# Six more attention heads with scores split in two terms, and the weights' low parts moved from GpSimd to VectorE

## The chip, the cores and the metric

The kernel runs on one core of a Trainium2 chip. Its engines are TensorE (PE in the profile, with PEld for its weight loads), VectorE (DVE), ScalarE (ACT), GpSimd (POOL) and SyncE (SP, which issues most DMAs here). Each engine has its own queue of instructions, and the engines wait for one another through semaphores. The metric is the device time of one execution in microseconds; lower is better.

## The reference

Eight batches of eight heads of causal attention with a decay, over 576 positions with 64 elements a head, then one two-layer network over all 4608 rows. All of it is in float32.

```python
scores = scale * np.matmul(q, k.transpose(0, 1, 3, 2))
cum = np.cumsum(np.log(np.clip(f, 0.0001, 1.0)), axis=-1)
scores = np.where(causal, -1e9, scores + cum[..., :, None] - cum[..., None, :])
attn = exp(scores - max(scores)) / (sum + 1e-09)
x = matmul(attn, v)                      # 64 heads of 576 x 64, heads side by side: 4608 x 512
h = np.maximum(x @ w_in, 0.0)            # w_in 512 x 2048, given as float64
out = h * h @ w_out                      # w_out 2048 x 512, given as float64
```

The kernel receives the two weight matrices as float64 words and turns them into float32 itself.

## The kernel before

**Attention.** A head is worked in six *units* (score tiles: keys in tiles of 128 on the partitions, queries along the free axis, in the shapes 128x320, 128x320, 128x192, 66x64, 128x448 and 128x256). The program runs over *slots*, one unit of one head each: 64 heads x 6 units, with some slots ahead of the first head. In a slot stand, in this order: the unit's `score` matmuls with the exponential on ScalarE (`p`), the product of `p` with `v` for the unit of two slots before (`av_part`), the steps of the division (`finish`), and then twice (half 0 and half 1 of the slot): events with due times, a stretch of weight conversion (`cv`), and as many halves of a network step as `fill` says are due. The events of half 0 stand ahead of the first stretch and those of half 1 ahead of the second.

**Maxima.** A softmax needs each query's maximum ahead of its scores. `max_units(h)` computes rough scores one head ahead, in six pieces: one matmul of the rounded q (`r2`, the stationary operand) and rounded k (`kl0`), and one reduction on VectorE that writes the negative maximum per query. The table `MAXIMA` holds their slots, for whole and for split heads.

**Whole and split heads.** `NWHOLE` says which heads are *whole*: for these, q and k are loaded twice by DMA (rounded on the way into `rk` by `load_rounded`, and as they are into `rl` by `load_whole`), a unit's scores are one float32 matmul pair (two records in the profile), the mask is added by a small bf16 matmul, `p` and `v` are used as float32, and the six maxima are gathered in a column tile, turned into a row by five small matmuls and copied by ScalarE (`turn_maxima`). For the *split* heads, q and k come once as `qkraw`; `prep` makes rounded high parts and low parts (the remainder, another subtraction), a unit's scores are two single-pass matmuls in fp32r (high by high with the decay and maximum rows, and a second one over 128 rows that holds both cross terms), the maxima go to their row by small DMAs, and `p` and `v` are split too, with three matmuls each. Before the change, heads 0 to 15 are whole and heads 16 to 63 are split.

**Weights.** `weight_ops` converts 32 tiles of 128x512 weights in four yields each: VectorE clips and shifts the exponent and joins the words (lines 228, 233, 236 and 240), ScalarE makes the magnitude (line 205) and the rounded high part (line 210), and GpSimd subtracts it for the low part (line 216, one yield ahead of line 240 of the following tile). `RATES` gives yields per slot.

**Network.** A step of it has two halves. `mlp1` multiplies a chunk of 256 rows by one tile of `w_in` (12 matmuls, line 555), then ScalarE makes relu and square (`r`, `gh`) and VectorE the exact square and its low part (`g`, `gl`). `mlp2` multiplies by a tile of `w_out` (6 matmuls, line 578), one step behind. The network of a batch of heads runs in between the attention of the next batch, so that of batch 0 runs beside heads 8 to 15; after the last head only network is left. When the second chunk of rows begins, scores and maxima share two PSUM banks; before that they have four.

**Order.** `in_order` ties PE, ACT, DVE and POOL to the order in which the program was traced; SP's DMAs are placed by the scheduler. So on these four an instruction that waits holds up all that stands behind it.

## Time and profile before

| | us |
|---|---|
| time, median of 3 runs | 1220.62 (1219.54 to 1220.74) |
| profiled execution, its own time | 1217.56 |
| its span, first to last instruction | 1215.8 |
| mean granted TensorE clock | 0.994 of full speed |
| busy: PE, DVE, ACT, POOL | 1189.4, 769.5, 706.2, 361.8 |

By place of the span: up to about 95 us only attention and weight conversion run (heads 0 to 8); from there to about 230 us heads 9 to 15 with the network of batch 0 and the rest of the conversion; then heads 16 to 63 with the network of the batch before; from about 1057 us only network. In rows of instructions, the first number is the start in us from the span's beginning, the second how long the record lasts; successive records of one engine overlap, so that the cost of one is read from its start to the start of the next. "x2" joins two records. A bracket at a row's end gives how long the engine sat idle ahead of it, and what ended that.

### The profile page before, as it was taken

Reading aid. Unit: us, or ns where it says so; the run is one execution under the profiler, and the core shown is the slowest. Engines: PE = TensorE matmul, PEld = TensorE weight load, DVE = VectorE, ACT = ScalarE, POOL = GpSimd, SP = SyncE. Lnnn points to the kernel's source line nnn. Section 1 sums busy time; section 2 is a strip of 40 time slices with the busy share of each in tenths; the row PEclk is TensorE's granted clock in tenths of the full one; section 3 lists DMA queues with packets and bytes.
Section 4 is the critical chain, followed back from the end, with each engine's and each line's share of the span. In section 5 each row is a group of like instructions: output and inputs, shape, how many; then the busy total and the mean of one; then the engine's idle time right before and its main releaser. Section 6 shows DMA issues by size and latency. Waiting matters only on the chain.

```text
span 1215.8 us, 23255 instructions
## 1 busy us (share of the span) xinstructions
PE 1189.4 (98%) x7816; PEld 1047.3 (86%) x7816; DVE 769.5 (63%) x2031; ACT 706.2 (58%) x1736; POOL 361.8 (30%) x551
## 2 busy tenths in 40 slices
PE   6999999899999999999999999999999999999998
PEld 3668787779999898999999989988999899999997
DVE  5767776766767667665655766667676767533332
ACT  3875556566666666655556566666666666533232
POOL 3332322333334333322322333333333333200000
PEclk8999999999999999999999999999999999999999
DMA  7889310111211112111121212212121212000000
GB/s 217 206 198 272 90 42 26 47 46 42 59 42 53 38 47 50 41 49 27 43 55 21 53 32 44 57 42 58 37 50 33 58 43 58 12 28 11 9 18 18
DMA packets 104767, 72.16 MB, mean 59 GB/s; under 512 B 86573, under 2 KB 86573, under 8 KB 104649
## 3 DMA queue, kind: packets, MB, share of 16 engines
q1 hardware_dynamic: 103368, 65.96, 21.2%
q0 software_dynamic: 1280, 4.72, 1.6%
q8 instruction: 62, 1.02, 0.4%
q14 instruction: 57, 0.46, 0.1%
HBM read 60.51 MB, written 9.87 MB: 58 GB/s over the span
## 4 chain that ended last, share of the span: by engine, by line
PE 90%; ACT 4%; DVE 2%; issue 2%; DMA 1%; POOL 0%; SPq 0%; DVEq 0%; POOLq 0%; ACTq 0%
PE bank L555 33%; PE bank L578 31%; PE bank L346 4%; PE bank L392 3%; PE bank L435 3%; PE bank L456 3%; PE bank L402 3%; PE bank L437 3%; PE bank L436 3%; PE bank L399 3%; ACT r L563 1%; DVE bank L354 1%; ACT gh L565 0%; ACT den L471 0%; ACT p L409 0%
## 5 line engine op out<-in xcount | busy, mean ns | idle before, releaser
L578 PE MATMUL bank<-w,gh 128*128 128x512 f32 x1152 | 414.1, 400 | 0.0
L555 PE MATMUL bank<-xh,w 128*128 128x256 f32 x2304 | 329.0, 285 | 1.9 <-POOL w L216 1.9
L555 PEld LDWEIGHTS bank<-xh,w 128*128 128x128 f32 x2304 | 300.3, 189 | 10.3 <-POOL w L216 2.4
L425 DVE TENSOR_TENSOR pl<-p,ph 128x320 fp32r<-128x320 f32 (+4 forms) x288 | 177.4, 616 | 192.8 <-ACT ph L424 188.3
L578 PEld LDWEIGHTS bank<-w,gh 128*128 128x128 f32 x1152 | 217.5, 189 | 38.4
L563 ACT ACTIVATE r<-bank 128x256 f32<-128x256 f32 x288 | 110.6, 384 | 218.4 <-PE bank L555 172.3
L578 PE MATMUL bank<-w,gl 128*128 128x512 f32 x576 | 226.9, 394 | 0.2 <-DVE gl L566 0.2
L564 DVE TENSOR_TENSOR g<-r 128x256 f32<-128x256 f32 x288 | 125.7, 437 | 146.6 <-ACT r L563 146.0
L424 ACT CAST ph<-p 128x320 fp32r<-128x320 f32 (+4 forms) x288 | 119.4, 415 | 145.6 <-POOL p L411 103.0
L411 POOL TENSOR_SCALAR_AFFINE_SELECT p<-p 128x128 f32<-128x128 f32 (+1 forms) x240 | 77.1, 321 | 412.0 <-ACT p L409 317.6
L555 PE MATMUL bank<-xl,w 128*128 128x256 f32 x1152 | 184.5, 282 | 0.0
L555 PEld LDWEIGHTS bank<-xl,w 128*128 128x128 f32 x1152 | 158.2, 191 | 0.2 <-DVE xl L543 0.2
L566 DVE TENSOR_TENSOR gl<-g,gh 128x256 fp32r<-128x256 f32 x288 | 130.3, 452 | 36.2 <-ACT p L409 2.0
L354 DVE CUSTOM_DVE_ANT_0 bank<-bank,mz 128x256 f32<-128x256 f32 (+4 forms) x320 | 133.4, 433 | 22.6 <-PE bank L346 20.5
L409 ACT ACTIVATE p<-bank 128x320 f32<-128x320 f32 (+4 forms) x288 | 111.6, 388 | 60.1 <-PE bank L402 48.9
L565 ACT ACTIVATE gh<-r 128x256 fp32r<-128x256 f32 x288 | 120.6, 419 | 9.4
L346 PE MATMUL bank<-rk 66*128 66x320 f32 (+4 forms) x384 | 110.6, 317 | 13.9 <-DVE tcol L354 11.0
L578 PEld LDWEIGHTS bank<-w,gl 128*128 128x128 f32 x576 | 109.3, 190 | 14.4 <-DVE gl L566 0.9
L435 PE MATMUL bank<-pl,vh 128*65 128x320 f32 (+4 forms) x336 | 93.3, 278 | 2.6 <-ACT den L471 2.6
L346 PEld LDWEIGHTS bank<-rk 66*128 66x128 f32 (+1 forms) x384 | 67.2, 181 | 29.3 <-DVE tcol L354 13.0
L436 PE MATMUL bank<-ph,v 128*64 128x320 f32 (+4 forms) x336 | 91.2, 271 | 0.0
L437 PE MATMUL bank<-ph,vh 128*65 128x320 f32 (+4 forms) x336 | 89.3, 272 | 0.0
(92 smaller groups left out, 1539.0 us busy)
## 6 DMA issues: line engine op xcount, KB each, us to landing
qkraw<-in_qk SPq DMA_DIRECT2D x48, 288.0 KB
v<-in_v SPq DMA_DIRECT2D x64, 160.0 KB
out<-osb SPq DMA_DIRECT2D x36, 256.0 KB
den<-rdr SPq DMA_DIRECT2D x62, 144.0 KB
w<-in_w_in SPq DMA_DIRECT2D x16, 512.0 KB
w<-in_w_out SPq DMA_DIRECT2D x16, 512.0 KB
rl<-in_qk SPq DMA_DIRECT2D x16, 288.0 KB
rk<-in_qk POOLq DMA_DIRECT2D x16, 288.0 KB, 4.4
```

What stands on the lines that cost most here:

```text
L346: nc.tensor.matmul(ps[:m, :n], st["r2"][:D + 2, q0:q0 + m], st["kl0"][:D + 2, k0:k0 + n], start=True, stop=True,)
L354: nc.vector.tensor_tensor_reduce(out=ps[:m, :n], in0=ps[:m, :n], in1=mz[:m, mo:mo + n], op0=ALU.add, op1=ALU.min, scale=-1.0, scalar=init, ...
L425: nc.vector.tensor_tensor(out=pl[:kn, :n], in0=p[:kn, :n], in1=ph[:kn, :n].bitcast(F32), op=ALU.subtract,)
L435: nc.tensor.matmul(acc[:D + 1, o], vh, pl[:kn, i], start=first, stop=False)
L436: nc.tensor.matmul(acc[:D, o], vl, ph[:kn, i], start=False, stop=False)
L437: nc.tensor.matmul(acc[:D + 1, o], vh, ph[:kn, i], start=False, stop=last)
L555: nc.tensor.matmul(ph[:, :T], w[:, s, cc], x[:, cc, :], start=(cc == 0 and k == 0), stop=(cc == NCC - 1 and k == 2),)
L563: nc.scalar.activation(out=r, in_=ph[:, :T], func=AF.Relu)
L564: nc.vector.tensor_tensor(out=g, in0=r, in1=r, op=ALU.mult)
L565: nc.scalar.activation(out=gh, in_=r, func=AF.Square)
L566: nc.vector.tensor_tensor(out=gl, in0=g, in1=gh.bitcast(F32), op=ALU.subtract)
L578: nc.tensor.matmul(po, g[:, ts], w[:, s], start=(fc == 0 and k == 0), stop=(fc == NF - 1 and k == 2),)
```

## The change

Heads 10 to 15 become a third kind. They have split scores like the later heads (`prep`, two matmuls a unit, maxima by small DMAs, and the later due times of `MAXIMA`: from slot 1.5 to slot 4 of the head before, where whole heads have slot 0 to slot 2.5), but `p` and `v` stay whole and the mask is added by a matmul, as in whole heads. Their `prep` differs from that of the later heads: the rounded k (part 0, slot 0.5) and the rounded q (part 1, slot 1.5) are cast by ScalarE straight into `rk`, copied from there into `rl` by a DMA from SBUF to SBUF, and both low parts are subtracted on VectorE (parts 2 and 3, slots 1.5 and 3.5). The old `prep`, with the casts for `rk` on VectorE at slot 0.5 and the low parts on GpSimd, is now `prep_split` and serves heads 16 to 63. In the weight conversion, the low part moves from GpSimd to VectorE and one yield later, behind line 240.

```diff
-    NWHOLE = 16
+    NWHOLE = 10
+    NPLAIN = 16
...
         def low_part(i):
...
-                nc.gpsimd.tensor_tensor(out=hl[:, 1], in0=w, in1=hl[:, 0].bitcast(F32), op=ALU.subtract)
+                nc.vector.tensor_tensor(out=hl[:, 1], in0=w, in1=hl[:, 0].bitcast(F32), op=ALU.subtract)
...
             nc.vector.scalar_tensor_tensor(wi, high, -0x40000000, wi, ALU.bitwise_and, ALU.bitwise_or)
-            low_part(i - 1)
             magnitude(i + 1)
             yield
             nc.vector.scalar_tensor_tensor(wi, low, 29, wi, ALU.logical_shift_right, ALU.bitwise_or)
+            low_part(i - 1)
...
     def prep(h, part):
+
+        if h >= NPLAIN:
+            prep_split(h, part)
+            return
+        if part == 0:
+            x = planes(wk, F32R, "rl")
+            (r2, kl0), (r1, l2) = ((x.q, x.k) for x in (rounded[h % 2], x))
+            st = state[h] = dict(r2=r2, kl0=rounded[h % 2].k, r1=r1, l2=l2, p={}, raw=raws.pop(h))
+            load_cum(h, kl0)
+            nc.gpsimd.memset(f32(x.k[:, S:]), 0.0)
+            nc.scalar.copy(out=kl0[:D, :S], in_=st["raw"][:, 1, :])
+            nc.sync.dma_start(out=f32(l2[D:, :S]), in_=f32(kl0[:D, :S]))
+        st = state[h]
+        q, k = (st["raw"][:, i, :] for i in range(2))
+        if part == 1:
+            nc.scalar.copy(out=st["r2"][:D], in_=q)
+            nc.sync.dma_start(out=f32(st["r1"][:D]), in_=f32(st["r2"][:D]))
+        if part == 2:
+            nc.vector.tensor_tensor(
+                out=st["l2"][:D, :S], in0=k, in1=st["kl0"][:D, :S].bitcast(F32), op=ALU.subtract,
+            )
+        if part == 3:
+            nc.vector.tensor_tensor(out=st["r1"][D:], in0=q, in1=st["r2"][:D].bitcast(F32), op=ALU.subtract)
+
+    def prep_split(h, part):
...
+        masked = q0 == k0
+        added = masked and h < NPLAIN
         if h < NWHOLE:
...
+            nc.tensor.matmul(ps[:kn, :n], k[:, k0:k0 + kn], r[:, q0:q1], start=True, stop=not added)
         else:
...
             nc.tensor.matmul(
-                ps[:kn, :n], st["l2"][:, k0:k0 + kn], st["r1"][:, q0:q1], start=False, stop=True,
-            )
-        if h < NWHOLE:
+                ps[:kn, :n], st["l2"][:, k0:k0 + kn], st["r1"][:, q0:q1], start=False, stop=not added,
+            )
+        m = min(kn, n)
+        if added:
+            nc.tensor.matmul(
+                ps[:kn, :m], mz[:kn, MW - P:MW - P + kn], eye[:kn, :m], start=False, stop=True,
+            )
+        if h < NPLAIN:
             p = wk.tile([P, 448], F32, name=("ph", "pl")[u % 2], bufs=3)
```

`split_v`, the choice of matmul in `av_part`, the column of ones in `load_v` and the splitting of `p` ask for `NPLAIN` where they asked for `NWHOLE`.

How the instructions stand now, in slot 1 of head 10 (its second unit), in which the first maximum piece of head 11 is due. ScalarE before, from the relu of the `mlp1` ahead of that unit (L563 and L565 are relu and square, L409 the exponential, L470 and L471 copy a finished head's sum out, L205 and L210 belong to the weights):

```order
L210 CAST w_1395<-osb 128x512
L563 ACTIVATE r<-bank_1397 128x256
L565 ACTIVATE gh<-r 128x256
L409 ACTIVATE pl<-bank_1418 128x320
L470 COPY xt_1159<-bank_1423 64x256
L471 COPY den<-bank_1423 1x256
L205 ACTIVATE wmag<-w_1213 128x512
L409 ACTIVATE ph<-bank_1450 128x192
```

ScalarE in the change, the same place (L590 and L592 relu and square, L436 the exponential, L497 and L498 the copies out, L206 and L211 the weights; L317 and L322 are the two new casts):

```order
L317 CAST rk_80<-qkraw 64x576
L211 CAST w_1393<-osb 128x512
L590 ACTIVATE r<-bank_1395 128x256
L592 ACTIVATE gh<-r 128x256
L436 ACTIVATE pl<-bank_1416 128x320
L497 COPY xt_1155<-bank_1422 64x256
L498 COPY den<-bank_1422 1x256
L206 ACTIVATE wmag<-w_1204 128x512
L322 CAST rk_80<-qkraw 64x576
L436 ACTIVATE ph<-bank_1450 128x192
```

The cast of k stands ahead of the weight cast, and that of q, which the first maximum piece needs, last of what the slot gives ScalarE.

TensorE before, from the `mlp1` in slot 0 (L555) over the unit's scores (L392), the mask (L395) and `av_part` (L456) to the maximum pieces of head 11 (L346) and the `mlp2` behind them (L578):

```order
L555 MATMUL bank_1397<-xl_1114,w_972 128x256 x4
L392 MATMUL bank_1418<-rl 128x320
L395 LDWEIGHTS mz
L395 MATMUL bank_1418<-p,mz 128x128
L456 MATMUL bank_1423<-pl,v 65x256
L456 MATMUL bank_1423<-ph,v 65x128
L346 MATMUL bank_1431<-rk_80 128x448
L346 MATMUL bank_1438<-rk_80 128x320
L578 MATMUL bank_1215<-w_895,gh 128x512
```

TensorE in the change (L582 `mlp1`, L421 and L424 the two score matmuls, L429 the mask, L483 `av_part`, L372 the maximum piece, L605 `mlp2`):

```order
L582 MATMUL bank_1395<-xl_1111,w_970 128x256 x4
L421 MATMUL bank_1416<-rk_79 128x320
L424 MATMUL bank_1416<-rl 128x320
L429 LDWEIGHTS mz
L429 MATMUL bank_1416<-p,mz 128x128
L483 MATMUL bank_1422<-pl,v 65x256
L483 MATMUL bank_1422<-ph,v 65x128
L372 MATMUL bank_1437<-rk_80 128x256
L605 MATMUL bank_1206<-w_895,gh 128x512
```

The pieces of head 11 that stood here were its third and fourth; now its first stands here, behind `av_part` and ahead of `mlp2`.

VectorE in the change, the same slot and the one after (L237, L240, L229 and L234 convert weights, L217 is the moved low part, L325 the low part of head 11's k, L380 the reductions of the maxima):

```order
L237 SCALAR_TENSOR_TENSOR osb<-w_1116,osb 128x512
L325 TENSOR_TENSOR rl<-qkraw,rk_80 64x576
L380 ISA bank_1437,tcol<-bank_1437,mz 128x256
L380 ISA tcol 128x1
L240 SCALAR_TENSOR_TENSOR osb<-w_1116,osb 128x512
L217 TENSOR_TENSOR w_1393<-osb,w_1393 128x512
L380 ISA bank_1458,tcol<-bank_1458,mz,tcol 128x320
L380 ISA tcol 128x1
L229 TENSOR_SCALAR wmag<-wmag 128x512
L380 ISA bank_1466,tcol<-bank_1466,mz 128x448
```

Two subtractions now stand between or ahead of the reductions, where before only lines 228 to 240 did.

More of the change, by code (lines that the diff above doesn't have):

```diff
@@ L326, in split_v @@
     def split_v(h):
-        if NWHOLE <= h < NH:
+        if NPLAIN <= h < NH:
             st = state[h]
@@ L388, in score @@
         ps = bank("s")
+        masked = q0 == k0
+        added = masked and h < NPLAIN
         if h < NWHOLE:
-            masked = q0 == k0
             r, k = st["whole"].q[:D + 3], st["whole"].k[:D + 3]
-            nc.tensor.matmul(ps[:kn, :n], k[:, k0:k0 + kn], r[:, q0:q1], start=True, stop=not masked)
-            if masked:
-                m = min(kn, n)
-                nc.tensor.matmul(
-                    ps[:kn, :m], mz[:kn, MW - P:MW - P + kn], eye[:kn, :m], start=False, stop=True,
-                )
+            nc.tensor.matmul(ps[:kn, :n], k[:, k0:k0 + kn], r[:, q0:q1], start=True, stop=not added)
         else:
@@ L402, in score @@
             nc.tensor.matmul(
-                ps[:kn, :n], st["l2"][:, k0:k0 + kn], st["r1"][:, q0:q1], start=False, stop=True,
+                ps[:kn, :n], st["l2"][:, k0:k0 + kn], st["r1"][:, q0:q1], start=False, stop=not added,
             )
-        if h < NWHOLE:
+        m = min(kn, n)
[3 more added lines that the diff above has]
+            )
+        if h < NPLAIN:
             p = wk.tile([P, 448], F32, name=("ph", "pl")[u % 2], bufs=3)
@@ L409, in score @@
         nc.scalar.activation(out=p[:kn, :n], in_=ps[:kn, :n], func=AF.Exp, scale=SCALE)
-        if h >= NWHOLE and q0 == k0:
+        if masked and not added:
             nc.gpsimd.affine_select(
-                out=p[:kn, :min(kn, n)], in_=p[:kn, :min(kn, n)], pattern=[[1, min(kn, n)]],
+                out=p[:kn, :m], in_=p[:kn, :m], pattern=[[1, m]],
                 compare_op=ALU.is_ge, fill=0.0, base=0, channel_multiplier=-1,
@@ L453, in av_part @@
         o, i = slice(s0 - base, s1 - base), slice(s0 - q0, s1 - q0)
-        if h < NWHOLE:
+        if h < NPLAIN:
             vr = st["vr"][:kn, j, :D + 1]
@@ L747, in decay_attention_relu2_kernel @@
             score(h, u)
-            if h >= NWHOLE:
+            if h >= NPLAIN:
                 unsplit.append((h, u))
```

## The prediction

> **What bounds the kernel now.** I read the page's busy shares first, then the table by windows, then TensorE's own waits in the timeline.
>
> ```profile
> PE 1189.4 (98%) x7816; PEld 1047.3 (86%) x7816; DVE 769.5 (63%) x2031; ACT 706.2 (58%) x1736; POOL 361.8 (30%) x551
> 95.00:230.00 135.00, 129.05 (x796) 105.07 (x795) 100.96 (x231) 77.44 (x187) 39.28 (x38) 1.00 0.33 94
> ```
>
> The second row is the stretch in which heads 9 to 15 run beside the network (length, then busy time of PE, PEld, DVE, ACT and POOL, clock, DMA share, GB/s). TensorE is at its limit there as in the whole span: 129.05 of 135 us, DVE at 101 and ACT at 77. All of the change for heads 10 to 15 lies in this stretch. So a microsecond of TensorE work taken out is a microsecond gained, and a microsecond for which TensorE is made to wait is one lost. The waits that TensorE has there now are few:
>
> ```profile
> 139.95 0.35 PE L346 MATMUL bank<-rk 66*128 66x192 f32 x1 [1.28 <-DVE p L354]
> 201.22 0.24 PE L377 MATMUL bank<-p 128*65 128x64 f32 x1 [1.27 <-ACT ph L409]
> 227.32 1.21 PE L555 MATMUL bank<-xh,w 128*128 128x256 f32 x8 [1.89 <-POOL w L216]
> 252.32 0.41 PE L346 MATMUL bank<-rk 66*128 66x320 f32 x1 [2.16 <-DVE tcol L354]
> ```
>
> **TensorE work that goes.** Successive records overlap, so I take each cost from start to start.
>
> ```profile
> 117.77 0.70 PE L392 MATMUL bank<-rl 67*128 67x320 f32 x2
> 118.31 0.22 PE L395 MATMUL bank<-p,mz 128*128 128x128 bf16 x1
> 118.37 0.60 PE L456 MATMUL bank<-pl,v 128*65 128x256 f32 x2
> 118.80 0.38 PE L456 MATMUL bank<-ph,v 128*65 128x128 f32 x2
> 118.94 0.60 PE L346 MATMUL bank<-rk 66*128 66x448 f32 x2
> ...
> 125.42 0.92 PE L392 MATMUL bank<-rl 67*128 67x448 f32 x2
> 126.18 0.22 PE L395 MATMUL bank<-p,mz 128*128 128x128 bf16 x1
> ...
> 126.43 0.57 PE L377 MATMUL bank<-p 128*65 128x128 f32 x5
> 126.83 1.19 PE L555 MATMUL bank<-xh,w 128*128 128x256 f32 x8
> ...
> 128.34 0.40 PE L578 MATMUL bank<-w,gh 128*128 128x512 f32 x1
> ...
> 129.73 0.60 PE L392 MATMUL bank<-rl 67*128 67x256 f32 x2
> ...
> 238.74 0.37 PE L399 MATMUL bank<-rk 67*128 67x448 f32 x1
> ...
> 239.15 0.25 PE L435 MATMUL bank<-pl,vh 128*65 128x192 f32 x1
> ...
> 244.20 0.31 PE L399 MATMUL bank<-rk 67*128 67x320 f32 x1
> ...
> 244.49 0.31 PE L435 MATMUL bank<-pl,vh 128*65 128x320 f32 x1
> ```
>
> A whole unit of 320 columns takes 118.31 - 117.77 = 0.54 us and one of 448 takes 0.76, both 1.69 ns a column. A split one (both matmuls) takes 0.29 and 0.41, some 0.91 ns a column. A head has 1600 columns: 2.71 against 1.46 us, less a little for its 64-column unit, so 1.2 us a head and 7.1 for six. `turn_maxima` goes: its five matmuls take 126.83 - 126.43 = 0.40 us, 2.4 for six heads. **Together 9.5 us.** Mask, `av_part` and maxima stay as many as they were. Two prices for later from the same rows: `mlp1` 1.51 us (1.45 to 1.5), `mlp2` 129.73 - 128.34 = 1.39 us.
>
> **Waits that go.** The 1.27 us before line 377 go with `turn_maxima`. The 1.28 us come from a VectorE that ran late while GpSimd subtracted a low part, and go with that. Rows of the two engines show how:
>
> ```profile
> 104.97 1.29 POOL L216 TENSOR_TENSOR w<-osb,w 128x512 fp32r<-128x512 f32 x1 [5.12 <-ACT w L210]
> 105.17 1.37 DVE L233 TENSOR_SCALAR osb<-wmag 128x512 int32<-128x512 int32 x1
> 110.20 0.42 DVE L233 TENSOR_SCALAR osb<-wmag 128x512 int32<-128x512 int32 x1
> ```
>
> The same instruction takes 0.42 us alone and 1.37 us beside GpSimd's subtraction. Of the 1.89 us at 227.32, where the last tiles' low parts queue on GpSimd, I let 1.1 go, since on VectorE the same part still has line 240 ahead of it. **Together 3.6 us** (bounds 1.3, the one that cannot stay, and 4.4).
>
> **The wait that comes.** The first maximum piece needs the rounded q. The due table calls part 1 of `prep` and that piece in the same half-slot, and the cast now stands on ScalarE behind all else of the slot. TensorE is in order, so that piece holds up everything behind it. What ScalarE does there is timed in the same slot of the run before:
>
> ```profile
> 118.03 0.39 ACT L563 ACTIVATE r<-bank 128x256 f32<-128x256 f32 x1 [1.51 <-PE bank L555]
> 118.45 0.42 ACT L565 ACTIVATE gh<-r 128x256 fp32r<-128x256 f32 x1
> 118.77 0.42 ACT L409 ACTIVATE pl<-bank 128x320 f32<-128x320 f32 x1
> 119.22 0.36 ACT L470 COPY xt<-bank 64x256 f32<-64x256 f32 x1
> 119.60 0.36 ACT L471 COPY den<-bank 1x256 f32<-1x256 f32 x1
> 119.98 0.68 ACT L205 ACTIVATE wmag<-w 128x512 f32<-128x512 f32 x1
> L315 ACT CAST rl<-qkraw 64x576 fp32r<-64x576 f32 x48 | 32.1, 670 | 0.7
> ```
>
> For head 11 the cast follows line 205: it would start at about 120.58, end 0.67 us later and release TensorE at 121.3. TensorE is done with `av_part` at 118.94, and 0.25 us sooner once the scores are split. So it waits 2.6 us; today it runs maxima there without one. The other heads, with the same prices and a weight cast or `wmag` at 0.6 us, from the end of the mask's issue: where `mlp1` precedes the unit, relu and square stand ahead of the exponential; where a network half stands between `av_part` and the piece, it covers 1.4 to 1.5 us.
> Head 10: ready after 3.0, TensorE there after 0.57 + 1.39: waits 1.06. Head 11: 3.17 against 0.57: 2.6. Head 12 (`mlp1` in between, whose own relu and square come ahead of the cast): 3.73 against 2.02: 1.7. Head 13: 2.13 against 0.57: 1.56. Head 14: 3.92 against 1.96: 1.96. Head 15: 3.17 against 0.57: 2.6. **Sum 11.5 us** (bounds: nothing, if ScalarE were ahead each time; 15, six times the longest).
>
> **The clock.** The profile shows half clock after one short stall of this kind and none after another:
>
> ```profile
> 225.90:229.30 3.40, 1.98 (x15) 1.96 (x16) 3.40 (x4) 3.04 (x7) 2.88 (x3) 1.00 0.21 48
> 249.80:253.20 3.40, 1.24 (x10) 0.92 (x9) 2.76 (x6) 1.49 (x4) 1.73 (x2) 1.00 0.02 3
> 250.00:260.00 10.00, 7.84 (x43) 6.83 (x42) 6.51 (x17) 3.77 (x11) 3.19 (x4) 0.83 0.16 54
> ```
>
> In the first 3.4 us TensorE is busy for 1.98 and the clock stays; in the second for 1.24, around the wait of 2.16 us, and the 10 us around it have a clock of 0.83: 1.7 us of work lost. Waits of 2.6 us (heads 11 and 15) and 1.96 (head 14) lie beyond or at that point, depending on where they fall. I take **two such losses, 3.4 us** (bounds 0 and 5.1, three). [...]
>
> **VectorE.** It gains 32 low parts and 12 low parts of q and k and loses its collisions with GpSimd.
>
> ```profile
> L543 DVE TENSOR_TENSOR xl<-xt,xh 128x512 fp32r<-128x512 f32 x4 | 2.8, 693 | 0.1
> L170 DVE TENSOR_TENSOR qkraw<-xt,qkraw 64x576 fp32r<-64x576 f32 x1 | 0.8, 751 | 0.0
> L233 DVE TENSOR_SCALAR osb<-wmag 128x512 int32<-128x512 int32 x19 | 12.8, 673 | 0.6
> L564 DVE TENSOR_TENSOR g<-r 128x256 f32<-128x256 f32 x28 | 13.4, 479 | 25.7 <-ACT r L563 25.5
> ```
>
> Within the stretch, some 20 x 0.69 + 12 x 0.75 = 23 us are added. Line 233 alone is 19 x (0.673 - 0.42) = 4.8 us dearer there than undisturbed; with the other three conversion lines about 10 us are given back. Net 13 us on 101 of 135, while 25.5 us of its idle time is waiting for relu. Most is hidden there; the subtractions stand ahead of reductions that free PSUM banks, two in the later part. I take **1.5 us** (bounds 0, and 13 if none is hidden), near the 1.28 us that a late VectorE costs in this stretch today.
>
> **At nothing.** The 12 copies by DMA and the 30 small maxima DMAs: first scores come two to five slots (6 to 14 us) later; a late one would stop a head's first unit. 24 loads become 6 with as many bytes less. SP's later weight loads now queue behind these, but conversion stages four tiles ahead. The 14 copies out of ScalarE's `turn_maxima` go, 12 casts come; its 58 idle us in the stretch cover them, but for their place, which is priced above. GpSimd's 32 subtractions leave; TensorE waited for them only at 227.32. Ahead of 95 us the low parts go to VectorE while it is not the limit (its half-us waits there may shift by as much). Behind 230 us nothing changes.
>
> **The sum.** -9.5 - 3.6 + 11.5 + 3.4 + 1.5 = +3.3 us, so 1217.56 becomes 1220.9 for the profiled execution. That execution ran 3.1 us below the median of the timed runs (1220.62), on which I put the same difference: **1223.9 us**.
>
> **The rivals.**
> *The waits cost no clock and are a little shorter.* The row at 225.9 speaks for it (a 1.89 us wait without loss), the row at 249.8 against. [...] Without the 3.4 us: -0.1, so 1220.5. Within 0.2% (2.4 us), which is about what a measurement of this kernel can tell from no change.
> *The cast is in time.* Faster. If ScalarE reaches the cast before TensorE reaches the piece (its idle time before relu in these rows, 1.51 us at 118.03, shows that it is not backlogged), the 11.5 and the 3.4 us go: -11.6, so 1209. If half is hidden, 1214. It decides at each head whether the chain behind the exponential is shorter than TensorE's work up to the piece; the rows give 2.1 to 3.9 against 0.6 to 2.0, so I find it unlikely.
> *VectorE becomes the bound.* If none of its 13 us is hidden, +3.3 - 1.5 + 13 = +14.8, less what lies under the waits for the cast: about 1230. Its 25.5 us of waiting speak against it.
> *The split does not pay on TensorE.* If the second matmul's weight loads showed, the 7.1 us would shrink; heads 16 on show split pairs at 0.29 us back to back, so I leave this to the range.
>
> **How the numbers follow.** Forecast case 0.45 (alone 1221 to 1227); no clock loss 0.28; cast in time, fully or by half, 0.19; VectorE 0.08. Slower by over 0.2%: 0.47; within: 0.30; faster: 0.23, which has in it the case by halves and errors of the sum. For the range I leave out the full hiding and the worst of VectorE: 1212 to 1230.
>
> **What would show it.** Right: six waits of 1 to 2.6 us at the first maximum piece (line 372 of the changed kernel), put down to the ScalarE cast of line 322; clock below 1.00 near heads 11 and 15; split units at 0.29 us for 320 columns; no 1.37 us records of the conversion lines; DVE busy near 114 us in the stretch. Wrong: no wait at line 372 (then 1209 to 1214), or waits named VectorE above a few us (then towards 1230).

## The result, and the profile after

| | before | after |
|---|---|---|
| median, us (4 runs each) | 1220.68 (1219.54 to 1222.2) | 1230.84 (1230.44 to 1231.17) |
| profiled execution | 1217.56 | 1230.44 |
| span | 1215.8 | 1228.7 |
| mean granted clock | 0.994 | 0.990 |

The change makes the kernel slower: ratio 1.0092, 95% interval [1.0072, 1.0111], +10.2 us by the medians. The forecast was +3.3 us.

The busy shares on the page of the changed kernel:

```profile
PE 1184.8 (96%) x7786; PEld 1044.3 (85%) x7786; DVE 783.2 (64%) x2075; ACT 708.1 (58%) x1736; POOL 317.2 (26%) x519
```

TensorE is less busy (1189.4 before) in a longer span, so the time is in waits. All of TensorE's waits of half a microsecond and more between 95 and 300 us, from its timeline:

```profile
102.40 0.39 PE L372 MATMUL bank<-rk 66*128 66x256 f32 x1 [0.96 <-ACT rk L322]
120.99 0.38 PE L372 MATMUL bank<-rk 66*128 66x256 f32 x1 [2.28 <-ACT rk L322]
139.57 0.39 PE L372 MATMUL bank<-rk 66*128 66x256 f32 x1 [1.54 <-ACT rk L322]
157.33 0.39 PE L372 MATMUL bank<-rk 66*128 66x256 f32 x1 [1.52 <-ACT rk L322]
167.13 0.24 PE L372 MATMUL bank<-rk 66*64 66x64 f32 x1 [1.74 <-DVE tcol L380]
179.51 0.39 PE L372 MATMUL bank<-rk 66*128 66x256 f32 x1 [1.17 <-ACT rk L322]
197.86 0.38 PE L372 MATMUL bank<-rk 66*128 66x256 f32 x1 [2.24 <-ACT rk L322]
205.73 0.41 PE L372 MATMUL bank<-rk 66*128 66x320 f32 x1 [1.23 <-DVE tcol L380]
222.73 0.64 PE L372 MATMUL bank<-rk 66*128 66x320 f32 x1 [3.79 <-DVE tcol L380]
237.16 1.19 PE L582 MATMUL bank<-xh,w 128*128 128x256 f32 x8 [1.62 <-ACT w L211]
243.10 0.42 PE L372 MATMUL bank<-rk 66*128 66x320 f32 x1 [1.10 <-DVE tcol L380]
260.55 0.38 PE L372 MATMUL bank<-rk 66*128 66x256 f32 x1 [1.56 <-DVE rk L340]
263.87 0.64 PE L372 MATMUL bank<-rk 66*128 66x320 f32 x1 [2.21 <-DVE tcol L380]
```

They sum to 22.96 us; in the kernel before the same stretch has 8.24, in six rows. Two of these six, head 16's second piece and head 17's:

```profile
213.57 0.41 PE L346 MATMUL bank<-rk 66*128 66x320 f32 x1 [0.90 <-DVE tcol L354]
232.85 0.42 PE L346 MATMUL bank<-rk 66*128 66x320 f32 x1 [0.74 <-DVE tcol L354]
```

The 22.96 us are mainly of two kinds. The six rows with `ACT rk L322` are the predicted ones: each new head's first maximum piece waits for the cast of q (9.71 us). The rows with `DVE` are waits for a reduction to free a PSUM bank (the one at 260.55 for a cast of q or k): at 167 and 206 us in the maxima of heads 13 and 15, at 222.73 at head 16's second piece, then in the heads behind it. They sum to 11.63 us, against 5.35 before (1.28, 0.90, 0.74, 2.16 and one of 0.27, which is under the half microsecond and not in the 8.24). The one row left, 1.62 us for a cast of the weights, answers to the 1.89 us that the kernel before has at 227.32.

The timeline of VectorE and GpSimd ahead of the longest wait shows how it comes about:

```profile
217.95 1.89 DVE L217 TENSOR_TENSOR w<-osb,w 128x512 fp32r<-128x512 f32 x1
219.77 0.41 DVE L229 TENSOR_SCALAR wmag<-wmag 128x512 f32<-128x512 f32 x1
220.10 1.61 DVE L591 TENSOR_TENSOR g<-r 128x256 f32<-128x256 f32 x1
221.85 0.42 DVE L593 TENSOR_TENSOR gl<-g,gh 128x256 fp32r<-128x256 f32 x1
222.19 0.42 DVE L380 CUSTOM_DVE_ANT_0 bank<-bank,mz 128x256 f32<-128x256 f32 x1
```

```profile
213.81 1.44 POOL L519 TENSOR_TENSOR xt<-xt,den 128x576 f32<-128x576 f32 x1 [23.95 <-ACT r L590]
...
217.51 1.78 POOL L347 TENSOR_TENSOR rl<-qkraw,rk 64x576 fp32r<-64x576 f32 x1 [2.22 <-DVE rk L340]
219.62 1.81 POOL L350 TENSOR_TENSOR rl<-qkraw,rl 64x576 fp32r<-64x576 f32 x1 [0.33 <-ACT rl L344]
```

The low part of a weight tile (L217) ends 0.55 us behind GpSimd's first subtraction for head 16 (217.51 + 1.78 = 219.29), and `g` (L591) 0.28 us behind the second (219.62 + 1.81 = 221.43): both end only once GpSimd is done, after 1.89 and 1.61 us, where the same lines take 0.68 and 0.43 us at 209.45 and 210.52, with GpSimd idle. The reduction that frees the bank stands behind both.

The windows show the clock that was granted behind three of the waits (length, busy PE, PEld, DVE, ACT and POOL, granted clock, DMA share, GB/s):

```profile
95.00:240.00 145.00, 126.18 (x761) 103.08 (x760) 109.50 (x264) 78.94 (x184) 11.16 (x18) 0.96 0.30 81
167.91:171.32 3.41, 3.41 (x15) 3.02 (x14) 0.76 (x2) 0.69 (x1) 1.92 (x1) 0.50 0.36 87
198.63:202.04 3.41, 3.41 (x12) 2.48 (x11) 0.68 (x3) 0.33 (x1) 0.00 (x0) 0.50 0.19 43
222.52:225.94 3.42, 3.21 (x8) 2.64 (x9) 1.60 (x6) 0.68 (x1) 0.00 (x0) 0.50 0.37 86
```

Three stretches of 3.4 us at half clock stand in the stretch in which the kernel before has none; a fourth, at 263.5 us, answers to the one that it has at 253.2. Ahead of 95 us each kernel has three such pieces (at 17.7, 21.1 and 89.4 us before, at 14.3, 17.7 and 21.1 after). Three more cost 3 x 1.7 = 5.1 us. Only the one at 198.6 follows a wait for the cast; the others follow VectorE.

### The profile page after: what moved, and what is told of

It reads as the page before. It is cut to its first block, busy times and chain, and to the rows that moved or that the text cites. A ratio compares the mean times of both kernels' runs of the same rounds, so it can differ in the third digit from the quotient of the medians.

```text
span 1228.7 us, 23287 instructions
## 1 busy us (share of the span) xinstructions
PE 1184.8 (96%) x7786; PEld 1044.3 (85%) x7786; DVE 783.2 (64%) x2075; ACT 708.1 (58%) x1736; POOL 317.2 (26%) x519
## 4 chain that ended last, share of the span: by engine, by line
PE 64%; ACT 2%; issue 1%; POOL 1%; DVE 0%; DMA 0%; SPq 0%; POOLq 0%; DVEq 0%
PE bank L582 25%; PE bank L605 24%; PE bank L462 3%; PE bank L424 2%; PE bank L372 2%; PE bank L463 2%; PE bank L464 2%; PE bank L421 2%; ACT r L590 0%; ACT den L498 0%; ACT p L436 0%; POOL v L359 0%; ACT ph L451 0%; DMA den<-rdr 0%; ACT gh L592 0%
## 5 line engine op out<-in xcount | busy, mean ns | idle before, releaser
L605 PE MATMUL bank<-w,gh 128*128 128x512 f32 x1152 | 415.5, 401 | 0.0
L582 PE MATMUL bank<-xh,w 128*128 128x256 f32 x2304 | 330.2, 286 | 1.8 <-ACT w L211 1.6
L582 PEld LDWEIGHTS bank<-xh,w 128*128 128x128 f32 x2304 | 302.0, 190 | 10.5 <-ACT w L211 2.2
L605 PEld LDWEIGHTS bank<-w,gh 128*128 128x128 f32 x1152 | 218.1, 189 | 38.5
L590 ACT ACTIVATE r<-bank 128x256 f32<-128x256 f32 x288 | 110.6, 384 | 223.8 <-PE bank L582 187.8
L605 PE MATMUL bank<-w,gl 128*128 128x512 f32 x576 | 227.7, 395 | 0.2 <-DVE gl L593 0.2
L591 DVE TENSOR_TENSOR g<-r 128x256 f32<-128x256 f32 x288 | 128.7, 447 | 140.8 <-ACT r L590 140.1
L582 PE MATMUL bank<-xl,w 128*128 128x256 f32 x1152 | 184.6, 283 | 0.0
L582 PEld LDWEIGHTS bank<-xl,w 128*128 128x128 f32 x1152 | 158.4, 191 | 0.2 <-DVE xl L570 0.2
L380 DVE CUSTOM_DVE_ANT_0 bank<-bank,mz 128x256 f32<-128x256 f32 (+4 forms) x320 | 133.1, 432 | 23.9 <-PE bank L372 22.3
L593 DVE TENSOR_TENSOR gl<-g,gh 128x256 fp32r<-128x256 f32 x288 | 125.6, 436 | 35.4 <-DVE g L591 0.5
L436 ACT ACTIVATE p<-bank 128x320 f32<-128x320 f32 (+4 forms) x288 | 111.6, 388 | 61.6 <-PE bank L424 50.3
L372 PE MATMUL bank<-rk 66*128 66x320 f32 (+4 forms) x384 | 111.8, 320 | 32.1 <-DVE tcol L380 17.2
L592 ACT ACTIVATE gh<-r 128x256 fp32r<-128x256 f32 x288 | 120.5, 419 | 9.1
L605 PEld LDWEIGHTS bank<-w,gl 128*128 128x128 f32 x576 | 109.6, 190 | 14.7 <-DVE gl L593 1.1
L372 PEld LDWEIGHTS bank<-rk 66*128 66x128 f32 (+1 forms) x384 | 67.6, 182 | 51.1 <-DVE tcol L380 21.2
L424 PE MATMUL bank<-rl 128*128 128x320 f32 x324 | 95.3, 294 | 0.0
L421 PE MATMUL bank<-rk 67*128 67x320 f32 x324 | 93.4, 288 | 0.0
```

Source lines behind the costliest of these rows:

```text
L372: nc.tensor.matmul(ps[:m, :n], st["r2"][:D + 2, q0:q0 + m], st["kl0"][:D + 2, k0:k0 + n], start=True, stop=True,)
L380: nc.vector.tensor_tensor_reduce(out=ps[:m, :n], in0=ps[:m, :n], in1=mz[:m, mo:mo + n], op0=ALU.add, op1=ALU.min, scale=-1.0, scalar=init, ...
L421: nc.tensor.matmul(ps[:kn, :n], st["kl0"][:D + 3, k0:k0 + kn], st["r2"][:D + 3, q0:q1], start=True, stop=False,)
L424: nc.tensor.matmul(ps[:kn, :n], st["l2"][:, k0:k0 + kn], st["r1"][:, q0:q1], start=False, stop=not added,)
L582: nc.tensor.matmul(ph[:, :T], w[:, s, cc], x[:, cc, :], start=(cc == 0 and k == 0), stop=(cc == NCC - 1 and k == 2),)
L591: nc.vector.tensor_tensor(out=g, in0=r, in1=r, op=ALU.mult)
```

## The experiments

The experiments were timed in four batches (e, f, g and h), each beside the kernel before on one chip, and each batch on another chip; the ratios below are to the kernel before. So batches are compared by ratio, and times in microseconds only within a batch. The table has what decides in each: TensorE's waits of 0.5 us and more between 95 and 300 us of its profiled execution, by kind, and the number of 3.4 us pieces at half clock in that stretch.

| kernel | ratio, 95% interval | cast or row of a first piece | VectorE, heads 10 to 15 | head 16, second piece | all waits | half clock |
|---|---|---|---|---|---|---|
| before | 1 | 0 | 1.28 | 0.90 | 8.24 | 1 |
| after | 1.0092 [1.0072, 1.0111] | 9.71 | 2.97 | 3.79 | 22.96 | 4 |
| e1_low_gpsimd | 1.0103 [1.0068, 1.0139] | 9.75 | 3.69 | 3.09 | 22.97 | 6 |
| e2_low_alone | 0.9979 [0.9960, 0.9999] | 0 | 0.91 | 0.89 | 7.83 | 1 |
| e3_q_early | 1.0025 [1.0003, 1.0047] | 0 | 5.54 | 3.54 | 15.44 | 4 |
| e4_q_early_low_gpsimd | 1.0060 [1.0038, 1.0082] | 0 | 7.02 | 3.09 | 16.15 | 4 |
| f1_late_subtractions | 1.0025 [1.0003, 1.0046] | 0.66 | 3.74 | 3.49 | 13.93 | 2 |
| f2_rows_by_gpsimd_queue | 1.0026 [1.0003, 1.0050] | 0 | 5.15 | 2.98 | 15.65 | 2 |
| f4_subtractions_gpsimd | 1.0046 [1.0025, 1.0066] | 0 | 7.04 | 3.51 | 16.42 | 4 |
| f5_maxima_early | 1.0014 [0.9992, 1.0036] | 0 | 3.55 | 3.59 | 13.45 | 2 |
| g1_maxima_as_before | 1.0008 [0.9991, 1.0025] | 3.28 | 1.83 | 3.54 | 14.87 | 5 |
| g2_head16_late | 1.0023 [1.0008, 1.0038] | 0 | 5.43 | 3.54 | 15.66 | 3 |
| g3_g1_and_late | 1.0550 [1.0521, 1.0579] | 3.14 | 1.83 | 3.54 | 17.72 | 3 |
| h1_head16_on_vector | 1.0001 [0.9984, 1.0017] | 0 | 5.72 | 1.14 | 12.37 | 1 |
| h2_g1_row_by_gpsimd | 1.0000 [0.9987, 1.0012] | 2.58 | 1.87 | 3.54 | 14.31 | 3 |
| h3_both | 0.9972 [0.9955, 0.9989] | 2.99 | 1.83 | 1.35 | 12.58 | 2 |

The waits are of one execution, the ratios of four to twelve. The mean granted clock of the kernel before lay between 0.984 and 0.996 in its executions, and a half-clock piece is 0.0014 of it, so the number of pieces is that of one execution only. A ratio is the better witness of the whole, and a row the better one of a cause.

### The two parts of the change, and the place of the cast

**e1**: the changed kernel with the weights' low parts back on GpSimd, one yield earlier. **e2**: the kernel before with the low parts as the change has them, and nothing else. **e3**: the changed kernel with q cast and copied in part 0 of `prep`, a slot earlier. **e4**: e1 and e3 together.

```diff
 # e1 (e2 is the same edit of the kernel before, in reverse)
-                nc.vector.tensor_tensor(out=hl[:, 1], in0=w, in1=hl[:, 0].bitcast(F32), op=ALU.subtract)
+                nc.gpsimd.tensor_tensor(out=hl[:, 1], in0=w, in1=hl[:, 0].bitcast(F32), op=ALU.subtract)
...
+            low_part(i - 1)
             magnitude(i + 1)
             yield
             nc.vector.scalar_tensor_tensor(wi, low, 29, wi, ALU.logical_shift_right, ALU.bitwise_or)
-            low_part(i - 1)
 # e3
         if part == 0:
...
+            nc.scalar.copy(out=r2[:D], in_=st["raw"][:, 0, :])
+            nc.sync.dma_start(out=f32(r1[:D]), in_=f32(r2[:D]))
             nc.scalar.copy(out=kl0[:D, :S], in_=st["raw"][:, 1, :])
...
-        if part == 1:
-            nc.scalar.copy(out=st["r2"][:D], in_=q)
-            nc.sync.dma_start(out=f32(st["r1"][:D]), in_=f32(st["r2"][:D]))
```

> The changed kernel with the weights' low parts back on GpSimd, one yield earlier, as before the change; heads 10 to 15 stay split. Theory C (the late cast of q on ScalarE is the loss): the six waits at the first maximum piece stay at 9 to 10 us in sum, time 1228 to 1232. Theory V-w (the weights' low parts on VectorE are the other half of the loss: late reductions and collisions with GpSimd's remaining subtractions): the waits of TensorE on VectorE between 95 and 275 us fall from 11.6 us to about 5, and one or two half-clock stretches go with them: 1222 to 1226. Theory V-p (the twelve subtractions for q and k on VectorE are it): waits on VectorE stay above 9 us, time as under C.

> The kernel before with one change: the weights' low parts on VectorE, one yield later; all 16 heads whole. Theory C: 1218 to 1222, as before. Theory V-w: TensorE's waits on VectorE rise by some 4 to 6 us above the 5.4 us of before, 1224 to 1229. Theory V-p: no change, 1218 to 1222, or a little faster since conversion no longer collides with GpSimd.

> The changed kernel with the cast of q (and its copy by DMA) one slot earlier, in part 0 ahead of the cast of k. Theory C: the 9.7 us of waits at the first maximum piece go, and one half-clock stretch: 1218 to 1222. Theory V: VectorE is late anyway, the waits reappear at the second and later pieces put down to its reductions; no more than 4 us gained, 1226 to 1229.

> Both of the above: the cast of q early and the weights' low parts on GpSimd. Theories C and V-w together: all added waits go and the 9.3 us of TensorE work stay saved, 1209 to 1214. C without V-w: as e3, 1218 to 1222. V-p: waits on VectorE stay, 1216 to 1222.

The move of the low parts is no part of the loss: alone it gains a little (0.9979, the interval just under 1), and taken back it loses where the waits for the cast don't hide it (e4 against e3, 1.0060 against 1.0025). The place of the cast is a good half of the loss. In e3 all six waits for it are gone, and of +9.2 thousandths 2.5 are left. But the VectorE waits grow from 2.97 to 5.54 us in heads 10 to 15, since the waits for the cast had covered some. So the nine microseconds of TensorE work that the split saves are still eaten, by VectorE. TensorE's timeline in e3 around the first of those waits:

```profile
133.85 0.64 PE L581 MATMUL bank<-xl,w 128*128 128x256 f32 x4
134.33 0.28 PE L371 MATMUL bank<-rk 66*128 66x256 f32 x1
134.45 0.26 PE L420 MATMUL bank<-rk 67*128 67x192 f32 x1
...
134.73 0.70 PE L482 MATMUL bank<-ph,v 128*65 128x320 f32 x2
137.49 0.42 PE L371 MATMUL bank<-rk 66*128 66x320 f32 x1 [2.06 <-DVE tcol L379]
```

VectorE's over the same time:

```profile
135.25 0.56 DVE L590 TENSOR_TENSOR g<-r 128x256 f32<-128x256 f32 x1 [1.69 <-ACT r L589]
135.95 0.42 DVE L592 TENSOR_TENSOR gl<-g,gh 128x256 fp32r<-128x256 f32 x1
136.29 0.74 DVE L324 TENSOR_TENSOR rl<-qkraw,rk 64x576 fp32r<-64x576 f32 x1
136.97 0.42 DVE L379 CUSTOM_DVE_ANT_0 bank<-bank,mz 128x256 f32<-128x256 f32 x1
```

The piece at 134.33 stands directly behind an `mlp1`. Its reduction stands on VectorE behind `g` and `gl` of that `mlp1`, for which VectorE itself waits 1.69 us until relu has come. TensorE has one score unit and one `av_part`, some 1.1 us, until the next piece asks for a bank. The three other waits of e3 in heads 10 to 15, and the one at head 16's second piece:

```profile
162.27 0.24 PE L371 MATMUL bank<-rk 66*64 66x64 f32 x1 [1.74 <-DVE tcol L379]
175.36 0.41 PE L371 MATMUL bank<-rk 66*128 66x320 f32 x1 [0.51 <-DVE tcol L379]
196.41 0.41 PE L371 MATMUL bank<-rk 66*128 66x320 f32 x1 [1.23 <-DVE tcol L379]
213.15 0.63 PE L371 MATMUL bank<-rk 66*128 66x320 f32 x1 [3.54 <-DVE tcol L379]
```

Four things could be meant by "VectorE is late": the subtractions ahead of the reduction (theory P), the place of the pieces against the network's halves (M), GpSimd's divisions pushed into VectorE's way by SP's queue (S), and GpSimd's subtractions at head 16 (G).

### Which of the four

**f1**: e3 with parts 2 and 3 of `prep` behind the last maximum piece. **f2**: e3 with the small transfers of the maxima issued by GpSimd. **f4**: e3 with the 12 subtractions on GpSimd. **f5**: e3 with the pieces half a slot earlier.

```diff
 # f1
-                at((h - 1) * NU + SPLIT[part], 1, prep, h, part)
+                if h >= NPLAIN or part < 2:
+                    at((h - 1) * NU + SPLIT[part], 1, prep, h, part)
...
+        if NWHOLE <= h < NPLAIN:
+            for part in (2, 3):
+                at((h - 1) * NU + 4, 0, prep, h, part)
 # f2
-                nc.sync.dma_start(out=st["r2"].bitcast(F32)[D + 2:D + 3, q0:end], in_=acc)
+                eng = nc.gpsimd if h < NPLAIN else nc.sync
+                eng.dma_start(out=st["r2"].bitcast(F32)[D + 2:D + 3, q0:end], in_=acc)
 # f4 (for k, and the same for q)
-            nc.vector.tensor_tensor(
+            nc.gpsimd.tensor_tensor(
 # f5
+            x -= 0.5 * (NWHOLE <= h < NPLAIN)
             at((h - 1) * NU + int(x), int(2 * x) % 2, max_unit, h, i)
```

> e3_q_early with the two subtractions of heads 10 to 15 (k's and q's low parts, 12 operations of 0.4 to 0.75 us on VectorE) placed behind the head's last maximum piece instead of between the pieces. Theory P (the subtractions stand ahead of reductions on VectorE and make the pieces wait for a bank): the waits of e3_q_early at 137, 162, 175 and 196 us (2.06, 1.74, 0.51 and 1.23 us) go, with one half-clock stretch; about 5 us off, ratio to before 0.998 to 1.000. Theory M (the pieces come when VectorE is busy with the perceptron's g and gl, whatever else it has): at most 1 us off, ratio 1.0015 to 1.0035. The wait of 3.5 us at head 16's second piece is not touched by either.

> e3_q_early with the 36 small transfers of the maxima of heads 10 to 15 issued by GpSimd instead of SP. Theory S (the denominators' transfers stand on SP behind transfers that wait for a maximum, so the divisions by GpSimd at 210 to 220 us run beside VectorE's reductions and slow them): the wait of 3.5 us at head 16's second piece shrinks to under 1.5 us with its half-clock stretch, ratio 0.999 to 1.001. Rival: the collisions stay where they are, or GpSimd's sequencer, now held by the waiting transfers, makes the divisions later still: ratio 1.002 to 1.006.

> e3_q_early with the same 12 subtractions on GpSimd, where the kernel before has no such work for heads 10 to 15. Theory P: VectorE's chain is shorter by 0.4 to 0.75 us twice a head, waits at 137, 162, 175 and 196 us shrink, ratio 0.999 to 1.001. Rival (an operation of GpSimd beside one of VectorE costs VectorE more than the operation itself): the twelve run 1 to 2 us each and slow VectorE's by as much, ratio 1.003 to 1.008, as e4_q_early_low_gpsimd lost 0.4% by work of GpSimd.

> e3_q_early with the maximum pieces of heads 10 to 15 half a slot earlier (slots 1 to 3.5 instead of 1.5 to 4). Theory M (where the pieces stand against the perceptron's halves decides which of them waits for VectorE): the pattern of waits changes as a whole, the sum of the DVE waits between 130 and 200 us (5.5 us in e3_q_early) falls by 2 us or more, and the first pieces wait for the cast of q again by 0.3 to 1 us in some heads; ratio 0.999 to 1.003. Theory P: the subtractions stay between the pieces, and the waits stay within 1 us in sum; ratio 1.002 to 1.006.

Theory P falls short: with the subtractions out of the way the waits shrink by 1.8 us, not 5, and the ratio doesn't move. f2 does not test theory S, though head 16's wait stays at 2.98 us: GpSimd's division starts 8.69 us ahead of that piece (207.47 us) and in e3 8.50 us ahead (204.65), so the edit did not move it. The rows of e3 bound S instead. The division is over at 206.22 us, ahead of the two operations that are stretched there (208.37 and 210.53); it stretches only the `gl` before them, which takes 1.45 us at 205.06 and 0.42 alone (212.27). So S has at most about 1 us of that wait. On GpSimd the subtractions are dearer by the rows (7.04 us) and by the median (1.0046), as the rival had it, though the interval overlaps e3's. f5 lies between: the pattern of waits changes as M expected and loses 2.0 us, but the ratio alone (1.0014) is not told apart from e3's. So M was tried in full, and G with it.

**g1**: e3 with load, conversion and pieces of heads 10 to 15 one and a half slots earlier, so that the pieces stand where whole heads have them. **g2**: e3 with head 16's two subtractions on GpSimd called behind its last maximum piece. **g3**: g1, and g2's edit for all heads from 16 on.

```diff
 # g1
+        plain = NWHOLE <= h < NPLAIN
...
-            at((h - 2) * NU + LOAD, 0, load, h)
+            at((h - 2) * NU + LOAD - 2 * plain, int(plain), load, h)
             for part in range(4):
-                at((h - 1) * NU + SPLIT[part], 1, prep, h, part)
+                x = SPLIT[part] + 0.5 - 1.5 * plain
+                at((h - 1) * NU + int(x // 1), int(2 * x) % 2, prep, h, part)
...
-        for i, x in enumerate(MAXIMA[split]):
+        for i, x in enumerate(MAXIMA[split and not plain]):
 # g2
-                at((h - 1) * NU + SPLIT[part], 1, prep, h, part)
+                if part < 2 or not h == 16:
+                    at((h - 1) * NU + SPLIT[part], 1, prep, h, part)
...
+        if h == 16:
+            for part in (2, 3):
+                at((h - 1) * NU + 4, 0, prep, h, part)
```

> e3_q_early with the load, the conversion (all four parts) and the maximum pieces of heads 10 to 15 1.5 slots earlier, so that the pieces stand in slots 0 to 2.5 as in the kernel before. Theory M (a piece whose reduction stands on VectorE behind g and gl of a perceptron half that TensorE has only just finished makes the next piece wait 1.2 to 2 us; the later slots moved the pieces there): the VectorE waits between 130 and 200 us (5.5 us in e3_q_early) fall to 0.5 to 2.5 us and a half-clock stretch or two go, 4 to 7 us off, ratio 0.997 to 1.000; the wait at head 16's second piece stays. Rival (with less TensorE work in the heads VectorE itself is the bound, wherever the pieces stand): the sum stays over 4 us, ratio 1.001 to 1.004.

> e3_q_early with head 16's two subtractions on GpSimd placed behind its last maximum piece. Theory G (the wait of 3.54 us at head 16's second piece is made of VectorE operations stretched beside GpSimd's subtractions: 1.90 us for 0.68 and 1.61 us for 0.42): the wait shrinks to 1.0 to 1.6 us, the half-clock stretch there goes, 3 to 5 us off, ratio 0.998 to 1.000. Rival (VectorE's order there is late anyway): the wait stays over 2.5 us, ratio 1.002 to 1.003.

> g1_maxima_as_before and the two GpSimd subtractions of all heads from 16 on behind their last maximum piece. If M and G both hold: the waits at heads 10 to 16 sum to under 4 us, and the waits of heads 17 and 18 (1.12 and 2.19 us, where the kernel before waits too) shrink as well: ratio 0.990 to 0.995, under both kernels. If G fails, ratio as g1_maxima_as_before; if the late subtractions come too late for the heads' first scores, those wait for GpSimd by 0.5 to 2 us a head and the ratio is above that of g1_maxima_as_before.

g1 shows M in the rows: with the same operations on VectorE, its waits in heads 10 to 15 fall from 5.54 to 1.83 us. In head 12 a new wait stands ahead of them and can have covered some; in heads 13 to 15, which have none such, they fall from 3.48 to 0.81 us. In the time it is not told apart (1.0008 against 1.0025, with intervals that overlap), as the new wait took part of it. TensorE's timeline in g1:

```profile
133.98 0.82 PE L371 MATMUL bank<-rk 66*128 66x256 f32 x2 [3.28 <-DMA rk<-cum_dr]
143.24 0.36 PE L371 MATMUL bank<-rk 66*128 66x192 f32 x1 [1.02 <-DVE tcol L379]
173.72 0.41 PE L420 MATMUL bank<-rk 67*128 67x320 f32 x1 [0.81 <-DVE tcol L379]
```

The first row is head 12's first piece (the expectation of h2 calls it head 11's), which waits for the two rows of decay sums in k's plane; 6.8 us at half clock lie around it and behind it (133.0 to 139.8). g2 told nothing of G: GpSimd had nothing else to do, so it ran the two subtractions where it had run them before, at 208.86 and 211.23 us (207.92 and 210.29 in e3, where head 16's second piece is as much earlier). A later place in the program was no later place in time there, on an engine that only waited for data. g3 is 1.0550 [1.0521, 1.0579], a miss of both theories. The groups of instructions, of g3 and then of g1, show where its time goes (idle time before the group at the end):

```profile
L581 PE MATMUL bank<-xh,w 128*128 128x256 f32 x2304 | 334.6, 288 | 44.0 <-ACT r L589 41.7 <-ACT w L211 1.6
```

```profile
L581 PE MATMUL bank<-xh,w 128*128 128x256 f32 x2304 | 330.1, 286 | 1.9 <-ACT w L211 1.6 <-ACT r L589 0.3
```

`mlp1` waits for relu all through the later heads, 41.7 us for 0.3. A stretch of the trace shows a chain that makes relu late. In g3 GpSimd runs the two moved subtractions one behind the other (from 298.75 to 301.95 us); its masking of `p` stands behind them, at 303.22; ScalarE's cast of `p` waits 3.64 us for that, until 303.55 (1.76 us at the same place in g1), and relu stands right behind the cast, at 303.86. No run tested this.

**h1**: e3 with head 16's two subtractions on VectorE behind its last piece, so that they are off GpSimd for certain. **h2**: g1 with the rows of sums issued by GpSimd. **h3**: both.

```diff
 # h1 (with g2's edit; for k, and the same for q)
-            nc.gpsimd.tensor_tensor(out=l2, in0=k, in1=st["kl0"][:D, :S].bitcast(F32), op=ALU.subtract)
+            eng = nc.vector if h == 16 else nc.gpsimd
+            eng.tensor_tensor(out=l2, in0=k, in1=st["kl0"][:D, :S].bitcast(F32), op=ALU.subtract)
 # h2
-            nc.sync.dma_start(out=f32(k[r:r + 2, :S]), in_=cum_dr[h])
+            eng = nc.gpsimd if NWHOLE <= h < NPLAIN else nc.sync
+            eng.dma_start(out=f32(k[r:r + 2, :S]), in_=cum_dr[h])
```

> e3_q_early with head 16's two subtractions on VectorE, behind its last maximum piece, instead of GpSimd. In g2_head16_late they had only moved in the program: GpSimd had nothing ahead of them and ran them at the same place (208.86 and 211.23 us). Theory G (the wait of 3.54 us at head 16's second piece is made of VectorE operations stretched beside these two subtractions, 1.90 for 0.68 us and 1.61 for 0.42): the wait shrinks to 0.9 to 1.6 us, the half-clock stretch there goes, 3 to 5 us off, ratio 0.998 to 1.000. Rival (VectorE's order there is late anyway): the wait stays over 2.5 us, ratio 1.002 to 1.004.

> g1_maxima_as_before with the transfers of the two rows of sums into k's plane (heads 10 to 15) issued by GpSimd instead of SP, where head 11's was issued at 128.27 us, behind the denominators' transfer (127.03 us), and made TensorE wait 3.28 us at 133.98. Theory M as of g1: that wait and the half-clock stretch behind it go, 5 to 7 us off g1, ratio 0.995 to 0.997. Rival (GpSimd's queue holds them behind its own waits, or another wait takes the place): a wait of over 1 us stays at the first pieces, ratio 0.999 to 1.002.

> h1 and h2 together. If M and G both hold: ratio 0.991 to 0.994, under the kernel before and under e2_low_alone, the cover of the cast, the pieces' places and the GpSimd collision being together what the change lost. If only M holds 0.995 to 0.997.

VectorE's timeline in h1, ahead of head 16's second piece:

```profile
213.27 0.68 DVE L217 TENSOR_TENSOR w<-osb,w 128x512 fp32r<-128x512 f32 x1
213.87 0.41 DVE L229 TENSOR_SCALAR wmag<-wmag 128x512 f32<-128x512 f32 x1
214.21 0.41 DVE L592 TENSOR_TENSOR g<-r 128x256 f32<-128x256 f32 x1
214.75 0.43 DVE L594 TENSOR_TENSOR gl<-g,gh 128x256 fp32r<-128x256 f32 x1
215.09 0.43 DVE L381 CUSTOM_DVE_ANT_0 bank<-bank,mz 128x256 f32<-128x256 f32 x1
```

And TensorE's row for that piece:

```profile
215.63 0.41 PE L373 MATMUL bank<-rk 66*128 66x320 f32 x1 [1.14 <-DVE tcol L381]
```

This is the same order as in the changed kernel, where the low part took 1.89 us and `g` 1.61: alone they take 0.68 and 0.41, and the wait is 1.14 us for 3.54 in e3. G holds for this wait. What is left of it is about what a division costs there: `gl` at 209.93 takes 1.47 us beside one, and 0.42 alone (206.60). That is read from the rows and was not tested. h2 doesn't get rid of its transfer: the rows come 2.58 us late from GpSimd as well, so that M's full gain was not seen. In h3 the two gains seem to add up: by the medians h1 lies 2.4 thousandths below e3, h2 2.5, and h3 5.3, and only h3's interval lies clear of e3's. It falls short of the 0.991 to 0.994 expected, but is under the kernel before, 0.9972 [0.9955, 0.9989], in a median of 1215.36 against 1218.80 us. Against e2 (0.9979), which has none of the six heads split, its lead is within the intervals. What it has lost against the full gain is in its rows: 2.99 us at head 12's first piece, which nothing here took away, and VectorE's waits behind head 16.

## Why the prediction was right and wrong

The direction was right and the mechanism it was put down to is there; the size was 10.2 us for 3.3. That mechanism alone would not have made a clear loss: the TensorE work, the waits that go and the cast as measured, with the one clock loss that follows the cast (1.7 us) and VectorE at the 1.5 us foreseen, come to +0.8 us. By its own terms, from the two profiled executions:

| term | predicted | measured |
|---|---|---|
| TensorE work that goes | -9.5 | -9.3 |
| waits that go | -3.6 | -2.8 |
| waits for the cast of q | +11.5 | +9.7 |
| clock | +3.4 | +5.1 |
| VectorE | +1.5 | +7.6 |
| sum | +3.3 | +10.3 |

**TensorE work** was right: a split unit of 320 columns takes 0.30 us from start to start.

```profile
117.52 0.31 PE L421 MATMUL bank<-rk 67*128 67x320 f32 x1
...
117.82 0.23 PE L429 MATMUL bank<-p,mz 128*128 128x128 bf16 x1
```

By head, the units sum to 1.57 us for 2.72, 6.9 us in six heads, and the five small matmuls' 2.4 us went.

**Waits that go**: the 1.27 and the 1.28 us went. The 1.28 us were put down to GpSimd's low parts, and that reading is doubtful: e2, with the low parts on VectorE and nothing else changed, still waits 0.91 us at the same piece of head 12 (140.68). The 1.89 us at 227.32 became 1.62 for a ScalarE cast of the weights: another engine was next, and 0.27 was gained where 1.1 was counted.

**The cast** came out head by head, in us: 1.06, 2.6, 1.7, 1.56, 1.96, 2.6 predicted and 0.96, 2.28, 1.54, 1.52, 1.17, 2.24 measured. e3, with the cast a slot earlier, has none of them, so its place makes them. The reading of ScalarE's order in one slot of the run before, with its durations, came within 0.4 us in all heads but the fifth.

**The clock** had the right size for one loss and the wrong places. Head 11 cost none, head 15 one, and the two others came from VectorE waits that the prediction did not have.

**VectorE is the step that failed.** The prediction counted its added work, net 13 us, against 25.5 us of idle time and called it mostly hidden: 1.5 us. The count was not the error. VectorE's busy time went from 100.96 us (95 to 230 us before) to 109.50 (95 to 240 us after), less than foreseen. But TensorE waits for one reduction at a time, and that has a place in VectorE's order. Three things moved the places, of which the first two were shown in the rows by taking them away. (1) The due times: the pieces of heads 10 to 15 now fall behind an `mlp1` whose `g` and `gl` must come first (g1: 5.54 to 1.83 us). In the changed kernel itself this is only 2.97 us, against the 1.28 that went, since the waits for the cast cover the rest. The prediction looked at the due times for the cast of q and never asked what they do to the reductions. (2) Head 16, which the change doesn't touch: its wait grew from 0.90 to 3.79 us, as two VectorE operations met GpSimd's subtractions in the order that the shorter heads left (h1: back to 1.14). In e2, with the same low parts on VectorE but whole heads, one of the two meets (1.91 us at 209.53), and the other runs clear (0.42 us at 211.84); the wait is 0.89. (3) Behind 230 us, where "nothing changes" was written, VectorE's waits went from 3.17 (with the one of 0.27) to 4.87 us. e2 has 4.58 us there with no edit but the low parts, and e4 3.99 with the six heads split and the low parts on GpSimd, so neither part is the cause alone; this third stays unsettled.

**The range** ended at 1230 since "the worst of VectorE" was left out. That case had been given 8 in 100 on the ground that VectorE idles, which is the same error. **The rival** "VectorE becomes the bound" named the right engine for the wrong reason: VectorE is busy for 109.50 of 145 us and bounds nothing as a whole. That its figure, about 1230, is close to the 1230.44 of the profiled execution is luck: it counts 13 us of unhidden work, where 7.6 us of waits came.

Two more things stay open. Why the rows of decay sums reach head 12 late in g1, h2 and h3, from SP as from GpSimd, was not taken apart. And the two profiled executions drift apart by some 2 us more in the stretch in which nothing differs: the same `mlp2` comes 11.05 us later at 277 us of the kernel before (288.35 for 277.30) and 13.13 us later near the end (1216.30 for 1203.17). This was not assigned; the medians differ by 2.7 us less than these two executions do.

## What to carry to other kernels

VectorE was busy for 109.50 of 145 us here, and 7.6 us of waits came all the same: idle time of a second engine hides added work only where the instruction that the bound engine waits for doesn't stand behind it. So when due times move, read for each moved instruction what stands ahead of its reader in that engine's order, and what that in turn waits for. And ask it also of the next stage, which nobody edited: a stage that ends sooner meets its neighbours' work at another point (head 16's second piece here, 0.90 to 3.79 us).

## What the runs showed of the hardware

**In these runs a wait cost clock by where it fell.** The half-clock pieces begin on a grid of 3.41 us (167.91, 198.63 and 222.52 lie 9 and 7 such steps apart). Windows on that grid in the changed kernel, each just ahead of a loss:

```profile
164.50:167.91 3.41, 1.67 (x10) 1.01 (x9) 3.07 (x10) 1.74 (x4) 0.00 (x0) 1.00 0.27 87
195.22:198.63 3.41, 1.17 (x7) 0.83 (x6) 2.07 (x7) 3.09 (x7) 0.00 (x0) 1.00 0.34 74
```

In e3, a window and the one behind it:

```profile
160.31:163.72 3.41, 1.67 (x9) 1.23 (x8) 3.24 (x10) 1.73 (x4) 0.23 (x1) 1.00 0.29 87
163.72:167.13 3.41, 3.41 (x18) 3.21 (x17) 0.12 (x1) 0.47 (x2) 1.40 (x1) 0.50 0.35 87
```

And in h1:

```profile
166.94:170.35 3.41, 1.71 (x9) 1.45 (x10) 3.12 (x9) 1.58 (x3) 0.52 (x1) 1.00 0.30 87
170.35:173.77 3.42, 3.42 (x26) 3.11 (x25) 1.32 (x3) 1.07 (x3) 1.28 (x3) 1.00 0.35 88
```

TensorE busy for 1.67 of 3.41 us is followed by half clock (the changed kernel and e3), busy for 1.71 is not (h1). The same wait of 1.74 us stands in all three windows (in h1's but for its first 0.04 us). On this grid, between 95 and 300 us of before, after, e3, g1, h1 and h3, every window at full clock that is busy for 1.67 us or less is followed by half clock, and every one that is busy for 1.71 us or more by full clock. Other runs blur it: in g2 a window busy for 1.70 us is followed by full clock (136.70:140.12), in f4 one busy for 1.88 by half clock (174.91:178.32), and in the kernel before, ahead of this stretch, one busy for all of its 3.41 (85.95:89.36). So it is an estimate from these windows that the clock turns at some 1.7 of 3.41 us in these heads, good to some 0.2 us, and busy time is not all that counts; what else does was not shown. A wait of 2.28 us (at 120.99, shared by two windows, busy for 1.99 and 2.55 us) cost no clock, and one of 1.74 us did. So the length of a wait alone doesn't tell its cost here.

**A later place in the program was not always later in time.** On GpSimd it was not at head 16, where that engine only waited for data (g2: 208.86 us for 207.92 in e3, 0.94 later, and so is the piece that waits). It was on VectorE (f1: head 12's first subtraction at 148.48 us, 136.29 in e3), and on GpSimd in the later heads, where it also masks `p` (g3: the mask at 303.22 us stands behind both subtractions, and the cast of `p` waits 3.64 us for it, 1.76 in g1).
